# An attention and gated-MLP kernel on one core: block 4's last corner is carried in block 3's empty corner, so that each head makes 12 transposes in place of 13

## The chip, the cores and the metric

The kernel runs on one core of one Trainium2 chip. The metric is the device time of one execution in microseconds (us). The core has five engines that matter here, each with a queue of its own that runs in order: TensorE (PE in the profile; its weight loads are listed apart as PEld), VectorE (DVE), ScalarE (ACT), GpSimd (POOL) and SyncE (SP), which issues all the DMAs.

## What is computed

Attention over 8 batches of 8 heads, each 576 tokens by 64, with a causal mask and a bias that falls with a running sum; then one gated MLP over all tokens of each batch. Cut to what matters:

```python
scores = scale * np.matmul(q, k.transpose(0, 1, 3, 2))
cum = np.cumsum(np.maximum(s, 0.0), axis=-1)
bias = -(cum[:, :, :, None] - cum[:, :, None, :])
scores = np.where(causal, -1000000000.0, scores + np.minimum(bias, 0.0))
attn = np.exp(scores - np.max(scores, axis=-1, keepdims=True))
attn = attn / (np.sum(attn, axis=-1, keepdims=True) + 1e-09)
x = np.matmul(attn, v)                  # heads joined: 8 x 576 x 512
h = gelu(x @ w_in)                      # 8 x 576 x 1024, halves u and v
v_s = w_sg @ (layernorm(v) * g_ln) + b_sg  # over the 576 tokens
return x + (u * v_s) @ w_out
```

## The kernel before

**Blocks of a head.** The 576 query rows of a head are cut into nine groups of 64 and gathered into five blocks, numbered 0 to 4. Block 0 has 64 rows, the others 128. Because of the causal mask, block `it` needs only `ITW[it]` key columns: 64, 192, 320, 448 and 576. Block 4 holds the two last groups of queries: its rows 0 to 63 are the last group and see all 576 keys, its rows 64 to 127 are the group before and see 512. So of the last 64 columns of block 4 only the upper half, 64 x 64, holds anything. This is the corner of which the change speaks. Block 3 is the other way round: its rows 0 to 63 see 384 keys, its rows 64 to 127 see 448. Its buffer is 512 wide (`PW`), with columns 448 to 511 set to zero once at the start. Block 0's 64 x 64 is already put into block 3's rows 0 to 63, columns 384 to 447.

**Steps of a head.** `scores` multiplies queries and keys on PE (lines 295, 297, 298), adds the mask and takes the row minimum on DVE (line 305), takes the exponential with its row sum on ACT (line 315), and calls `norm`. `norm` (lines 318 to 338) adds 1e-9 to the five columns of row sums on ACT (line 320), takes the reciprocal on DVE (line 321) and scales the blocks in the order 3, 0, 2, 1, 4. All of this scaling is on POOL (line 338), but for block 3 of the first 12 heads, which ACT scales (line 336). The scaled blocks stand in `pbuf`, two sets of buffers that heads use in turn.

`transposes` (lines 371 to 430) turns the scaled blocks over, 128 columns at a time, by TensorE transposes against an identity (line 377). It makes four groups for each head, of 4, 4, 2 and 3 transposes. Each group fills one PSUM bank of the tag `pt`, which has two. The last group transposes columns 512 to 575 of block 4 (64 columns, the only narrow transpose), 384 to 511 of block 3 and 384 to 511 of block 4, and then copies the bank out into the tile `pd`. In the first 12 heads (`h < NP`) `pd` is one float32 tile (`pdh`) that two DVE copies fill (lines 420, 421). In the other 52 heads every operand is split into a rounded high part and a low part: ACT casts the high parts (lines 425, 426), and DVE subtracts for the low parts (lines 427, 429).

`pv` (lines 432 to 481) multiplies the transposed blocks with the values: into the bank `xx` (lines 450, 468), and for block 0 into a bank `x0`, which is taken from the two of `pt` (lines 469, 472). The values lie in six tiles of 128 rows. Tile 4 holds the last 64 keys twice, one above the other, and tile 5 the first 64 keys twice.

**The MLP of a batch.** `ffn` splits the attention output and makes units of matmuls of the kinds v, u, s and o (lines 518, 582, 597, 616), whose results are treated by ACT, DVE and POOL. It runs while the next batch's heads run; behind the last batch it runs alone.

**Order.** The steps of heads and MLPs are issued by places in time that are written out by hand (`POS`, `F0`, `F6`, `F7`, `ORDER`). The order of the instructions in each engine's queue is then chosen by the framework, which runs its own model of the timeline over them (`schedule_with_timeline_sim=True`); it also places every wait.

Of the kernel before, what the change touches and what calls it, by code (L numbers as in the profile page):

```python
# [8 lines left out]
F32 = mybir.dt.float32  # L9
# [5 lines left out]
ALU = mybir.AluOpType  # L15

B, H, S, D = 8, 8, 576, 64
# [3 lines left out]
P = 128  # L21
NC = DM // P
NT = 4
REM = S - NT * P
# [35 lines left out]
def tile_attn_gmlp(  # L60
# [12 lines left out]
    nc = tc.nc  # L73
# [9 lines left out]
    def eng(key):  # L83
        return [{"s": nc.scalar, "g": nc.gpsimd, "v": nc.vector}[x] for x in ENG[key]]

    def split(hi, lo, src, eng_hi, eng_lo):
        if eng_hi is nc.scalar:
            nc.scalar.copy(out=hi, in_=src)  # L88
        elif eng_hi is nc.gpsimd:
            nc.gpsimd.tensor_scalar(out=hi, in0=src, scalar1=1.0, scalar2=1.0, op0=ALU.mult, op1=ALU.mult)  # L90
        else:
            nc.vector.tensor_copy(out=hi, in_=src)
        eng_lo.tensor_tensor(out=lo, in0=src, in1=hi.bitcast(F32), op=ALU.subtract)  # L93
# [33 lines left out]
    st = moe.tile([P, 5, BH], F32, name="st", tag="vt", bufs=2)  # L127
# [9 lines left out]
    for c0, n in ((0, 512), (512, REM)):  # L137
        ps = ps_sc.tile([P, 512], F32, name="cps", tag="sc")
        jn = NT if c0 == 0 else 5
        for j in range(jn):  # L140
            k = P if j < NT else REM
            o = max(0, j * P - c0)
# [33 lines left out]
    pbuf = []  # L176
    sums = []
    for i in range(2):
        t = const.tile([66, S], F32R, name=f"q2_{i}")
# [3 lines left out]
        for it in range(5):  # L183
            t = const.tile([P, PW[it]], F32, name=f"p_{i}_{it}")
# [4 lines left out]
        t = const.tile([P, 5], F32, name=f"sum_{i}")  # L189
# [128 lines left out]
    def norm(h, its, rs):  # L318
        c = slice(min(its), max(its) + 1)
        nc.scalar.activation(out=rs[:, c], in_=sums[h % 2][:, c], func=AF.Copy, bias=1e-9)  # L320
        nc.vector.reciprocal(out=rs[:, c], in_=rs[:, c])  # L321
        for it in its:
            r, w = ITR[it], ITW[it]
            p = pbuf[h % 2][it][0:r, 0:w]
            e = eng("n0" if h < NP else "n")[it]


            o = [(p, p, rs[0:r, it:it + 1])]
            if it == 0:
                o = [(pbuf[h % 2][3][0:64, 384:448], p, rs[0:64, 0:1])]  # L330
            elif it == 1:
                o = [(p[:, 0:P], p[:, 0:P], rs[:, 1:2]),
                     (pbuf[h % 2][2][64:P, 256:320], p[64:P, P:192], rs[64:P, 1:2])]
            for po, pi, f in o:
                if e is nc.scalar:
                    nc.scalar.activation(out=po, in_=pi, func=AF.Copy, scale=f)
                else:
                    e.tensor_scalar(out=po, in0=pi, scalar1=f, scalar2=1.0, op0=ALU.mult, op1=ALU.mult)  # L338
# [32 lines left out]
    def transposes(h):  # L371
        d = heads[h]
        pb = pbuf[h % 2]
        pt = {}

        def tr(ps, c, it, jb, n=P):
            nc.tensor.transpose(out=ps[0:n, c:c + P], in_=pb[it][:, jb:jb + n], identity=ident)  # L377

        def new(name, w):
            if h < NP:  # L380
                x = "hl"[h % 2]
                pt[name] = (att.tile([P, w], F32, name=name + x, tag=name + x, bufs=1),)
            else:
                pt[name] = tuple(att.tile([P, w], F32R, name=name + x, tag=name + x, bufs=1) for x in "hl")

        def evac(name, c0, ps, w, e=nc.scalar):
            if h < NP:
                o = pt[name][0][:, c0:c0 + w]
                (e.copy if e is nc.scalar else e.tensor_copy)(out=o, in_=ps[:, 0:w])  # L389
            else:  # L390
                hi, lo = (t[:, c0:c0 + w] for t in pt[name])
                split(hi, lo, ps[:, 0:w], nc.scalar, nc.vector)

        d["pt"] = pt
        t = ps_pt.tile([P, 512], F32, name="pt", tag="pt")
        for c, it in ((128, 3), (384, 2), (0, 1), (256, 4)):
            tr(t, c, it, 0)
        new("pa", 512)
        evac("pa", 0, t, 512)
        yield 0.43  # L400
        t = ps_pt.tile([P, 512], F32, name="pt", tag="pt")
        tr(t, 384, 3, 128)
        tr(t, 0, 3, 256)
        tr(t, 256, 2, 256)
        tr(t, 128, 4, 256)
        new("pb", 768)
        evac("pb", 0, t, 512, nc.vector)
        yield 0.43
        t = ps_pt.tile([P, 512], F32, name="pt", tag="pt")
        tr(t, 128, 2, 128)  # L410
        tr(t, 0, 4, 128)
        evac("pb", 512, t, 256)
        yield 0.43
        t = ps_pt.tile([P, 512], F32, name="pt", tag="pt")
        tr(t, 0, 4, 512, 64)
        tr(t, 64, 3, 384)
        tr(t, 192, 4, 384)
        if h < NP:
            pt["pd"] = (att.tile([P, 320], F32, name="pdh", tag="pdh", bufs=1),)
            nc.vector.tensor_copy(out=pt["pd"][0][0:64, 0:64], in_=t[0:64, 0:64])  # L420
            nc.vector.tensor_copy(out=pt["pd"][0][:, 64:320], in_=t[:, 64:320])
        else:
            hi, lo = pt["pd"] = tuple(att.tile([P, w], F32R, name="pd" + x, tag="pd" + x, bufs=1)
                                      for x, w in (("h", 320), ("l", 192)))
            nc.scalar.copy(out=hi[0:64, 0:128], in_=t[0:64, 0:128])
            nc.scalar.copy(out=hi[:, 128:320], in_=t[:, 128:320])
            nc.vector.tensor_tensor(out=hi[64:128, 0:128], in0=t[0:64, 0:128], in1=hi[0:64, 0:128].bitcast(F32),
                                    op=ALU.subtract)
            nc.vector.tensor_tensor(out=lo, in0=t[:, 128:320], in1=hi[:, 128:320].bitcast(F32), op=ALU.subtract)
        yield 0.35  # L430

    def pv(h):
        d = heads[h]
        pt = d["pt"]
        f32 = h < NP
        c, half = h % H // 2, h % 2
        key = (h // H, c)
        if key not in xr:
            xr[key] = moe.tile([P, S], F32, name="xr", tag="xr", bufs=8)
        xt = xr[key]  # L440
        parts = 1 if f32 else 2
        rows = D if f32 else P

        def st(jt):
            return d["v"][:, jt, :] if f32 else d["vs"][:, jt, :, :].rearrange("p a d -> p (a d)")

        xx = ps_x.tile([P, 512], F32, name="xx", tag="xx")

        def mm(o0, o1, jt, m, **kw):
            nc.tensor.matmul(xx[0:rows, o0:o1], st(jt), m, **{"start": False, "stop": False, **kw})  # L450

        m, pb, pd = pt["pa"], pt["pb"], pt["pd"]
        for k in range(parts):
            mm(0, 512, 0, m[k], start=(k == 0))
        yield 0.2
        for k in range(parts):
            mm(64, 512, 1, pb[k][:, 320:768])
        for k in range(parts):  # L460
            mm(128, 448, 2, pb[k][:, 0:320])
        yield 0.65
        mm(192, 384, 3, pd[0][:, 128:320])
        if not f32:
            mm(192, 384, 3, pd[1])
        x0 = ps_pt.tile([P, 512], F32, name="x0", tag="pt")
        if f32:
            nc.tensor.matmul(xx[0:rows, 256:320], st(4)[0:REM], pd[0][0:REM, 0:64], start=False, stop=True)
            nc.tensor.matmul(x0[0:rows, 0:64], st(0), pd[0][:, 64:128], start=True, stop=True)
        else:  # L470
            mm(256, 320, 4, pd[0][:, 0:64], stop=True)
            nc.tensor.matmul(x0[:, 0:64], st(5), pd[0][:, 64:128], start=True, stop=True)
        hs = slice(64 * half, 64 * half + 64)
        for ps, o, sl in ((x0, slice(0, 64), slice(0, 64)), (xx, slice(0, 512), slice(64, S))):
            if f32:
                nc.scalar.copy(out=xt[hs, sl], in_=ps[0:64, o])
            else:
                nc.scalar.copy(out=xt[hs, sl], in_=ps[64:128, o])
                nc.vector.tensor_tensor(out=xt[hs, sl], in0=ps[0:64, o], in1=xt[hs, sl], op=ALU.add)
        del heads[h]  # L480
        yield 0.5
# [154 lines left out]
    def advance(g, h):  # L636
        if h not in g[1]:
            g[1][h] = g[0](h)
        next(g[1][h], None)

    sc, tr, pp = (scores, {}), (transposes, {}), (pv, {})
    for h in range(BH):
        if h > 0:
# [81 lines left out]
```

## Time and profile before

| | |
|---|---|
| time, median of 3 runs | 828.37 us (827.84 to 835.08) |
| the profiled execution's own time | 830.48 us |
| its span, first to last instruction | 828.8 us |
| mean granted TensorE clock | 0.991 |
| busy, share of the span | PE 96%, PEld 84%, DVE 72%, ACT 70%, POOL 72% |
| instructions | 5161 matmuls, 5161 weight loads, 1806 on DVE, 1620 on ACT, 979 on POOL |

How to read it: the busy shares are of one profiled execution. A matmul's duration is modelled to the end of its pipeline, so that matmuls which follow each other overlap, and what one costs is read from the distance between starts. The chain of waits is followed back from the last instruction, at each step to what released it; its shares say which engine and which line the end of the program hung on.

### The profile page before, as it was taken

What the parts mean: (1) busy time and instruction counts of PE and PEld (TensorE: products, weight loads), DVE (VectorE), ACT (ScalarE), POOL (GpSimd) and SP (SyncE); (2) the same over time, 40 slices, a digit from 0 to 9 for tenths busy, and PEclk for the clock granted to TensorE, in tenths of its full rate; (3) what the DMA queues carried; (4) which work ended last, traced back from release to release, by engine and by line L of the source; (5) the groups of instructions that cost most, each with busy time, mean ns of one, the idle gap of its engine ahead of it and who ended that gap; (6) DMA issues with size and microseconds to landing.
All of it is one profiled execution on the core that took longest, in us unless ns stands there. A gap on an engine that the chain in (4) does not pass through costs nothing.

```text
span 828.8 us, 16733 instructions
## 1 busy us (share of the span) xinstructions
PE 792.6 (96%) x5161; PEld 696.1 (84%) x5161; DVE 597.9 (72%) x1806; ACT 576.5 (70%) x1620; POOL 595.1 (72%) x979
## 2 busy tenths in 40 slices
PE   6899999899999999999989999999999999999878
PEld 3355666889989998999979998899989998899778
DVE  5995468975787578966888577965888678963652
ACT  4787778775686678866878577866787677862430
POOL 4987668878677768796768778785778778872451
PEclk9999999999999999999999999999999999999989
DMA  7656553343442543444434453443444353400101
GB/s 210 215 158 181 148 139 84 86 105 100 116 106 74 128 125 86 108 121 126 112 82 104 115 139 90 113 109 96 119 119 103 100 152 93 98 26 23 35 8 57
DMA packets 69804, 89.29 MB, mean 108 GB/s; under 512 B 25954, under 2 KB 42212, under 8 KB 69716
## 3 DMA queue, kind: packets, MB, share of 16 engines
q1 hardware_dynamic: 69716, 88.23, 40.8%
q8 instruction: 41, 0.67, 0.4%
q14 instruction: 47, 0.39, 0.2%
HBM read 42.27 MB, written 9.73 MB: 63 GB/s over the span
## 4 chain that ended last, share of the span: by engine, by line
PE 73%; DVE 12%; DMA 5%; ACT 3%; issue 3%; POOL 2%; SPq 1%; DVEq 0%; POOLq 0%; ACTq 0%
PE om L616 12%; PE sm L597 11%; PE um L582 10%; PE xx L450 10%; PE vm L518 9%; PE pt L377 8%; PE sc L297 4%; PE sc L298 4%; DVE p L305 2%; DMA xq<-xs 2%; DMA q<-k 2%; PE sm L601 1%; PE sm L600 1%; DVE wbits L220 1%; DVE vm L504 1%
## 5 line engine op out<-in xcount | busy, mean ns | idle before, releaser
L338 POOL TENSOR_SCALAR p<-p,rs 128x448 f32<-128x448 f32 (+4 forms) x372 | 180.5, 499 | 29.1 <-DVE rs L321 9.6
L315 ACT ACTIVATE p<-p,mn 128x448 f32<-128x448 f32 (+4 forms) x320 | 177.9, 557 | 24.5 <-DVE mn L305 22.4
L305 DVE CUSTOM_DVE_ANT_0 p<-sc,mask 64x64 f32<-64x64 f32 (+4 forms) x320 | 126.2, 422 | 56.4 <-PE pt L377 31.0
L377 PE MATMUL pt<-ident,p 128*128 128x128 f32 (+1 forms) x832 | 137.2, 278 | 5.3 <-DVE pbl L389 2.6
L597 PE MATMUL sm<-ws,vn 128*128 128x288 f32 x768 | 130.3, 304 | 0.7 <-POOL vn L567 0.6
L93 POOL TENSOR_TENSOR k<-raw,k 128x576 fp32r<-128x576 f32 x56 | 80.3, 1433 | 66.7 <-ACT k L88 33.3
L582 PE MATMUL um<-xs,wi 128*128 128x288 f32 x768 | 123.4, 300 | 2.5 <-DVE u L504 2.4
L616 PE MATMUL om<-gt,wo 128*128 128x288 f32 x768 | 125.7, 298 | 0.0
L582 PEld LDWEIGHTS um<-xs,wi 128*128 128x128 f32 x768 | 108.9, 188 | 8.9 <-DVE u L504 4.0
L597 PEld LDWEIGHTS sm<-ws,vn 128*128 128x128 f32 x768 | 112.4, 192 | 3.3 <-DVE u L504 1.0
L377 PEld LDWEIGHTS pt<-ident,p 128*128 128x128 f32 (+1 forms) x832 | 96.8, 138 | 21.8 <-DVE pbl L389 5.4
L616 PEld LDWEIGHTS om<-gt,wo 128*128 128x128 f32 x768 | 110.6, 188 | 2.3
L518 PE MATMUL vm<-wi,xs 128*128 128x512 f32 x384 | 103.4, 399 | 0.0
L297 PE MATMUL sc<-k,q 128*128 128x448 f32 x336 | 100.8, 308 | 1.5 <-DVE mn L305 0.8
L298 PE MATMUL sc<-k,q 66*128 66x448 f32 x336 | 89.3, 298 | 0.6 <-DMA k<-cum 0.6
L88 ACT CAST pbh<-pt 128x512 fp32r<-128x512 f32 x104 | 48.9, 479 | 58.8 <-PE pt L377 58.8
L518 PEld LDWEIGHTS vm<-wi,xs 128*128 128x128 f32 x384 | 69.7, 189 | 14.9 <-POOL xs L93 1.6
L93 POOL TENSOR_TENSOR gt<-u,gt 128x288 fp32r<-128x288 f32 x64 | 50.7, 806 | 41.6 <-ACT gt L88 41.1
L297 PEld LDWEIGHTS sc<-k,q 128*128 128x128 f32 x336 | 60.8, 181 | 9.1 <-DVE mn L305 3.9
L93 DVE TENSOR_TENSOR pbl<-pt,pbh 128x512 fp32r<-128x512 f32 x104 | 56.5, 549 | 15.9 <-ACT pbh L88 15.9
L298 PEld LDWEIGHTS sc<-k,q 66*128 66x128 f32 x336 | 60.9, 181 | 5.9 <-issue 0.9
L88 ACT CAST k<-raw 128x576 fp32r<-128x576 f32 x56 | 37.6, 671 | 39.5 <-PE sc L297 33.8
(142 smaller groups left out, 1704.8 us busy)
## 6 DMA issues: line engine op xcount, KB each, us to landing
q<-k SPq DMA_DIRECT2D x168, 144.0 KB
raw<-in_kq SPq DMA_DIRECT2D x56, 288.0 KB
vr<-in_vp SPq DMA_DIRECT2D x52, 192.0 KB
out_t<-ot SPq DMA_DIRECT2D x64, 144.0 KB
k<-k SPq DMA_DIRECT2D x56, 144.0 KB
wraw<-in_w_in SPq DMA_DIRECT2D x16, 256.0 KB
kf<-in_kq SPq DMA_DIRECT2D x8, 288.0 KB
qf<-in_kq SPq DMA_DIRECT2D x8, 288.0 KB
```

The costliest lines, as they stand in the source:

```text
L88: nc.scalar.copy(out=hi, in_=src)
L93: eng_lo.tensor_tensor(out=lo, in0=src, in1=hi.bitcast(F32), op=ALU.subtract)
L297: nc.tensor.matmul(o, d["q1"][:, i0:i0 + r], d["k1"][:, j0:j1], start=True, stop=False)
L298: nc.tensor.matmul(o, q2[h % 2][:, i0:i0 + r], d["k2"][0:66, j0:j1], start=False, stop=True)
L305: nc.vector.tensor_tensor_reduce(out=pbuf[h % 2][it][0:r, j0:j1], in0=pst[0:r, c0:c0 + j1 - j0], in1=(mask2 if it in (2, 4) else mask)[0:r ...
L315: nc.scalar.activation(out=p, in_=p, func=AF.Exp, bias=d["mn"][0:r, it:it + 1], scale=-1.0, accum_out=sums[h % 2][0:r, it:it + 1])
L338: e.tensor_scalar(out=po, in0=pi, scalar1=f, scalar2=1.0, op0=ALU.mult, op1=ALU.mult)
L377: nc.tensor.transpose(out=ps[0:n, c:c + P], in_=pb[it][:, jb:jb + n], identity=ident)
L518: nc.tensor.matmul(ps[0:r], xs[c][:, xi, ts_], wi[:, c, wj, fs], start=(n == 0), stop=(n == 11))
L582: nc.tensor.matmul(ps[:, 0:CH], wi[:, c, wj, dt * P:(dt + 1) * P], xs[c][:, xi, cs], start=(n == 0), stop=(n == 11))
L597: nc.tensor.matmul(ps[:, 0:CH], vn[j][:, vi, ds_], ws[:, j, wj, cs], start=(n == 0), stop=False)
L616: nc.tensor.matmul(ps[:, 0:CH], wo[:, c, wj, ms], gt[ch, c][:, gi, :], start=(n == 0), stop=(n == 11))
```

## The change

In `norm`, block 4 is scaled in two pieces: columns 0 to 511 as before, and the 64 x 64 corner (rows 0 to 63, columns 512 to 575) by an ACT instruction that writes its result into block 3's buffer, rows 0 to 63, columns 448 to 511. In `transposes`, the transpose of block 4's last 64 columns is gone: the transpose of block 3's columns 384 to 511 brings the corner along, and it comes out on partitions 64 to 127 of the PSUM columns 64 to 127, below block 0. The copies out of the bank follow it. In the first 12 heads one DVE copy goes. In the other 52 heads the ACT casts have other shapes (64x64 and 128x256 for 64x128 and 128x192), and the DVE subtraction of 64x128 becomes two of 64x64. In `pv` the first 12 heads multiply the corner from partitions 64 to 127 and block 0 from partitions 0 to 63 alone (values tile 5 for tile 0). Nothing is pinned in the order of the instructions.

```diff
@@ norm
+            elif it == 4:
+                o = [(p[:, 0:512], p[:, 0:512], rs[:, 4:5]),
+                     (pbuf[h % 2][3][0:64, 448:512], p[0:64, 512:S], rs[0:64, 4:5])]
             for po, pi, f in o:
-                if e is nc.scalar:
+                if e is nc.scalar or it == 4 and pi.shape[1] == 64:
                     nc.scalar.activation(out=po, in_=pi, func=AF.Copy, scale=f)
                 else:
                     e.tensor_scalar(out=po, in0=pi, scalar1=f, scalar2=1.0, op0=ALU.mult, op1=ALU.mult)
@@ transposes
-        tr(t, 0, 4, 512, 64)
         tr(t, 64, 3, 384)
         tr(t, 192, 4, 384)
         if h < NP:
             pt["pd"] = (att.tile([P, 320], F32, name="pdh", tag="pdh", bufs=1),)
-            nc.vector.tensor_copy(out=pt["pd"][0][0:64, 0:64], in_=t[0:64, 0:64])
             nc.vector.tensor_copy(out=pt["pd"][0][:, 64:320], in_=t[:, 64:320])
         else:
...
-            nc.scalar.copy(out=hi[0:64, 0:128], in_=t[0:64, 0:128])
-            nc.scalar.copy(out=hi[:, 128:320], in_=t[:, 128:320])
-            nc.vector.tensor_tensor(out=hi[64:128, 0:128], in0=t[0:64, 0:128], in1=hi[0:64, 0:128].bitcast(F32),
+            nc.scalar.copy(out=hi[64:128, 0:64], in_=t[64:128, 64:128])
+            nc.scalar.copy(out=hi[:, 64:320], in_=t[:, 64:320])
+            nc.vector.tensor_tensor(out=hi[0:64, 0:64], in0=t[64:128, 64:128], in1=hi[64:128, 0:64].bitcast(F32),
+                                    op=ALU.subtract)
+            nc.vector.tensor_tensor(out=hi[64:128, 64:128], in0=t[0:64, 64:128], in1=hi[0:64, 64:128].bitcast(F32),
                                     op=ALU.subtract)
             nc.vector.tensor_tensor(out=lo, in0=t[:, 128:320], in1=hi[:, 128:320].bitcast(F32), op=ALU.subtract)
@@ pv
         if f32:
-            nc.tensor.matmul(xx[0:rows, 256:320], st(4)[0:REM], pd[0][0:REM, 0:64], start=False, stop=True)
-            nc.tensor.matmul(x0[0:rows, 0:64], st(0), pd[0][:, 64:128], start=True, stop=True)
+            nc.tensor.matmul(xx[0:rows, 256:320], st(4)[REM:P], pd[0][REM:P, 64:128], start=False, stop=True)
+            nc.tensor.matmul(x0[0:rows, 0:64], st(5)[0:REM], pd[0][0:REM, 64:128], start=True, stop=True)
```

## Prediction

> **What bounds the kernel now.** I read the busy shares first, then the chain of waits by engine, then by line.
>
> ```profile
> span 828.8 us, 16733 instructions
> PE 792.6 (96%) x5161; PEld 696.1 (84%) x5161; DVE 597.9 (72%) x1806; ACT 576.5 (70%) x1620; POOL 595.1 (72%) x979
> ...
> PE 73%; DVE 12%; DMA 5%; ACT 3%; issue 3%; POOL 2%; SPq 1%; DVEq 0%; POOLq 0%; ACTq 0%
> ```
>
> PE is busy nearly throughout and carries 73% of the chain that sets the end. ACT, DVE and POOL are each near 70% busy, so they have room for a little work. But 3% of the chain is ACT and 12% is DVE, so work added there isn't quite free. The chain by line says how much of it is transposes:
>
> ```profile
> by line: PE om L616 12.0%; PE sm L597 10.6%; PE um L582 9.7%; PE xx L450 9.6%; PE vm L518 9.2%; PE pt L377 8.2%; PE sc L297 4.3%; PE sc L298 4.2%; issue 2.7%; DVE p L305 2.0%; DMA xq<-xs 1.9%; DMA q<-k 1.6%; PE sm L601 1.2%; PE sm L600 1.2%
> ...
> L377 PE MATMUL pt<-ident,p 128*128 128x128 f32 x768 | 130.3, 278 | 3.2 <-DVE xr L479 0.9 <-DVE pbl L389 0.8 <-ACT p L336 0.7
> L377 PE MATMUL pt<-ident,p 128*64 128x128 f32 x64 | 17.7, 277 | 2.1 <-DVE pbl L389 1.8 <-DVE pbl L93 0.3
> ```
>
> The second form, 128*64, is the one that goes: 64 of 832. It is as long as the wide form (277 against 278 ns), since both stream 128 columns of the identity. But that is a pipelined duration; the price is the distance to the next start. Three groups of one head, on PE, with what follows each:
>
> ```profile
> 450.64 0.60 PE L377 MATMUL pt<-ident,p 128*128 128x128 f32 x4
> 450.99 0.39 PE L298 MATMUL sc<-k,q 66*128 66x320 f32 x1
> ...
> 452.88 0.38 PE L377 MATMUL pt<-ident,p 128*128 128x128 f32 x2
> 453.02 0.48 PE L450 MATMUL xx<-pal,vs 128*128 128x512 f32 x1
> ...
> 453.86 0.49 PE L377 MATMUL pt<-ident,p 128*64 128x128 f32 x3
> 454.11 1.04 PE L616 MATMUL om<-gt,wo 128*128 128x288 f32 x6
> ```
>
> From the first start to the next matmul: 0.14 us for two, 0.25 for three (the group that loses one), 0.35 for four. So each further transpose costs 0.10 to 0.11 us; I take 0.108. The narrow one fits the same line, so its shape costs nothing beside that.
>
> **What goes.** One transpose for each of 64 heads: 64 x 0.108 = 6.9 us if PE set the pace everywhere. It doesn't: the chain holds 8.2% x 828.8 = 68.0 us of transposes, which is 82 ns for each of the 832. By that, 64 x 0.082 = 5.2 us leave the chain, three quarters of the full price. The other quarter stands where the chain runs over DMA or another engine; there a faster PE only waits longer. I take 5.2, and keep 0 and 6.9 as its ends.
>
> The Trainium skill ("TensorE: Matmul & The Clock Gate", Back-to-back issue gap) gives about 81 ns for one weight load and matmul of 128 columns in a steady stream. By that page the full price would be an estimated 5.2 us, and 3.9 on the chain; the trace has 0.10 to 0.11 us between starts of these float32 transposes, and the measurement decides.
>
> **What is added.** No row shows a 64x64 scaling on ACT. The nearest:
>
> ```profile
> L336 ACT ACTIVATE p<-p,rs 128x448 f32<-128x448 f32 x12 | 8.0, 663 | 1.0 <-DVE rs L321 1.0
> L315 ACT ACTIVATE p<-p,mn 64x64 f32<-64x64 f32 x64 | 21.5, 336 | 0.0
> L478 ACT COPY xr<-xx 64x512 f32<-64x512 f32 x52 | 30.3, 582 | 1.3 <-PE xx L450 0.9
> L478 ACT COPY xr<-x 64x64 f32<-64x64 f32 x52 | 10.8, 208 | 12.0 <-PE x L472 11.1
> L425 ACT CAST pdh<-pt 64x128 fp32r<-64x128 f32 x52 | 13.1, 253 | 9.8 <-PE pt L377 9.1
> L426 ACT CAST pdh<-pt 128x192 fp32r<-128x192 f32 x52 | 16.4, 315 | 0.0
> L427 DVE TENSOR_TENSOR pdh<-pt,pdh 64x128 fp32r<-64x128 f32 x52 | 14.8, 284 | 3.5 <-ACT pdh L426 2.1
> L479 DVE TENSOR_TENSOR xr<-x,xr 64x64 f32<-64x64 f32 x52 | 11.0, 212 | 9.0 <-ACT xr L478 7.9
> L420 DVE COPY pdh<-pt 64x64 f32<-64x64 f32 x12 | 2.5, 208 | 0.0
> L338 POOL TENSOR_SCALAR p<-p,rs 128x576 f32<-128x576 f32 x64 | 49.0, 765 | 0.0
> L566 POOL TENSOR_SCALAR vt<-vt,rt 128x512 f32<-128x512 f32 x32 | 22.3, 695 | 11.0 <-ACT vn L564 11.0
> ```
>
> ACT: the same copy at 512 and at 64 columns takes 582 and 208 ns, 0.835 ns a column. The block scaling of 663 ns, cut by 384 columns, gives 342; the exponential of 64x64, with a per-row operand too, takes 336. I take 340 x 64 = 21.8 us, which brings ACT to 598, 72%. The casts change from 253 + 315 to about 208 (the 64x64 copy) + 368 (315 and 64 columns), some 10 ns more in 52 heads, 0.5 us. Of ACT's 576.5 busy us, 3% of the span, 24.9 us, stands in the chain, so a microsecond of ACT weighs 0.043: (21.8 + 0.5) x 0.043 = 1.0 us. The ends are 0 and all of it, 22.
>
> DVE: two subtractions of 64x64 in place of one of 64x128, by the 64x64 row 2 x 212 - 284 = 140 ns, x 52 = 7.3 us; less the copy, 12 x 208 = 2.5 us. That is 4.8 us more. DVE's weight is 0.12 x 828.8 / 597.9 = 0.166, so 0.8 us; ends 0 and 4.8.
>
> POOL: block 4 at 512 columns in place of 576 saves 70 ns x 64 = 4.5 us; its weight is 0.02 x 828.8 / 595.1 = 0.028, so -0.1 us. The narrower float32 multiplications of `pv` I put at 0, since these rows of 64 and 128 operand rows differ by 4 ns:
>
> ```profile
> L469 PE MATMUL x<-pdh,vf 128*64 128x64 f32 x24 | 3.9, 246 | 0.0
> L468 PE MATMUL xx<-pdh,vf 64*64 64x64 f32 x24 | 3.9, 242 | 0.0
> ```
>
> No DMA is issued more, less or later in its queue.
>
> **The waits that are added.** The transpose of block 3's last columns now waits for ACT's corner, and all of PE's queue behind it with it. One head shows the cover:
>
> ```profile
> 439.58 0.19 DVE L321 RECIPROCAL rs<-rs 128x5 f32<-128x5 f32 x1
> 440.59 3.46 POOL L338 TENSOR_SCALAR p<-p,rs 128x448 f32<-128x448 f32 x6
> ...
> 446.90 0.66 PE L377 MATMUL pt<-ident,p 128*128 128x128 f32 x4
> ```
>
> The reciprocal is there at 439.77, POOL scales until 444.05, and this head's first group starts at 446.90; the group that needs the corner is the one at 453.86. ACT has 14 us for 0.34 us of work, so PE's new wait costs nothing. Were that cover gone, PE would wait up to the 0.34 us in each head. The later subtraction in front of `pv` has a cover too:
>
> ```profile
> L427 DVE TENSOR_TENSOR pdh<-pt,pdh x52: 283/284/285, 148.6 to 760.1; 64x128 fp32r<-64x128 f32 x52
> ...
> who waited for it (us, times):
>   PEld x L472: 0.5, 1
>   PE x L472: 0.3, 1
> ```
>
> PE waited once in 52 heads for it, 0.3 us. With 0.14 us more it stays nearly always early. The bank is held 0.14 us longer as well, but all 832 transposes together had only 3.2 + 2.1 us of idle PE ahead of them.
>
> **The sum.** -5.2 + 1.0 + 0.8 - 0.1 = -3.5 us. Against the profiled execution's 830.48 us (span 828.8, with 1.7 around it) that is 827.0. This execution lay 0.25% above the median of 828.37, so against the median I say **824.9 us**, -0.4%. About 1% is what a measurement of this kernel can tell from no change.
>
> **The order is chosen anew.** The framework plans by its own model, and an instruction more on ACT and one less on PE can change its choices anywhere in the program. How much an order can be worth is seen inside this run. The same group of twelve matmuls opens each batch's stretch in the chain:
>
> ```profile
> 337.58 1.84 PE um L582 x12
> ...
> 433.48 1.85 PE um L582 x12
> ...
> 526.99 1.85 PE um L582 x12
> ...
> 620.63 1.85 PE um L582 x12
> ...
> 713.93 1.85 PE um L582 x12
> ```
>
> The stretches are 95.9, 93.5, 93.6 and 93.3 us, with eight heads and one MLP in each. So one order can cost 2.4 us a batch more than another; over the five batches from 246 to 714 us that is 12 us either lost, or, for the one slow stretch here, 2.4 us won.
>
> **The rivals.** *Nothing arrives* (0.2): the freed PE time turns into longer waits for DMAs and DVE, and the added 1.8 us of ACT and DVE stay: 830 us. For it speaks the 17% of the chain that DMA and DVE hold; against it, PE's 73%. The change not doing what it says is this case too: if the planner keeps a hole where the transpose stood, the time is the same.
>
> *All of it and more* (0.2): PE is the pace everywhere, the additions are covered: 828.4 - 6.9 = 821.5. With the slow stretch mended too it is 819.1, 1.1% faster. For it speaks PE's 96%, and that PE idled only 3.2 + 2.1 us ahead of all transposes. Against it, the chain holds 82 ns of each transpose and not 108, and each order that mends one stretch can spoil another.
>
> *ACT's queue is blocked* (0.15), on the other side. The corner needs the reciprocal, which is DVE's, and which itself needs ACT's sums. If the planner puts the corner right behind those sums, ACT stands until DVE comes to the reciprocal, and behind it stand the exponentials and the evacuations of PSUM that PE needs. The existing scaling does this:
>
> ```profile
> 65.83 0.20 ACT L320 ACTIVATE rs<-sum 128x5 f32<-128x5 f32 x1
> 66.06 0.19 DVE L321 RECIPROCAL rs<-rs 128x5 f32<-128x5 f32 x1 [2.51 <-ACT rs L320]
> 66.29 0.68 ACT L336 ACTIVATE p<-p,rs 128x448 f32<-128x448 f32 x1 [0.26 <-DVE rs L321]
> ```
>
> ACT idled 0.26 us for it here, with a DVE that was free at once. The Trainium skill (the same page, on engine queue depths) says that ACT and DVE are strictly first in, first out, and that only PE's weight loads pass ahead; the wait in this row agrees. A corner would block ACT for 0.26 + 0.34 = 0.60 us a head. It turns the sum at 5.2 / 64 = 0.08 us of that on the chain, and makes the kernel 1% slower at 0.21 us (13.5 us in all, of which 8.3 remain): 837 us. With all 0.60 it would be 38 - 5.2 = 33 us slower, 861. The same sign and size comes from the slow order in all batches (12 - 3.5 = 8.5 us), which is why I let 0.15 stand for both. Against it: the 14 us of room let the planner place the corner after the reciprocal.
>
> **How the numbers follow.** Forecast 0.45, nothing arrives 0.2, all and more 0.2, blocked 0.15. The forecast's own range is 822 to 829. For 8 in 10 I go from 818.5, below the second rival, to 836, leaving out most of the third. Faster by over 1% (under 820.1) needs all of the gain and a better order: 0.15 of the second rival's 0.2. Slower by over 1% (over 836.7) is the blocked ACT or the slow order in most batches: 0.13. Within 1%: 0.72.
>
> **What the profile after should show.** PE's transposes x768 and no 128*64 form; ACT with 64 new scalings of 64x64 at about 340 ns and little idle time ahead of them; POOL's block 4 at about 695 ns; DVE's 64x64 subtractions at about 212; the two-transpose group 0.14 us to the next start; steady stretches 8 x 0.108 = 0.9 us shorter, less 8 x 1.7 / 64 = 0.2 for what is added: about 92.8. PE idle ahead of the last group <-ACT would show the new wait, and stretches of 95 or 96 us a worse order. The prediction is wrong if order moves more than the 3.5 us of the sum.

## The result: 0.9% slower, and the profile after

The changed kernel takes 836.02 us (median of 20 runs, 831.37 to 840.84) against 827.88 for before (20 runs): 1.0091 times as long, 95% interval 1.0076 to 1.0106 (the two medians alone give 1.0098). The forecast was 0.4% faster. The page of the changed kernel has the span, the busy shares and the chain of waits by engine:

```profile
span 834.6 us, 16753 instructions
PE 791.4 (95%) x5097; PEld 693.6 (83%) x5097; DVE 604.4 (72%) x1846; ACT 599.6 (72%) x1684; POOL 590.9 (71%) x979
...
PE 71%; DVE 10%; DMA 8%; ACT 5%; issue 3%; POOL 2%; SPq 1%; POOLq 0%; DVEq 0%
```

64 matmuls are gone and PE's busy time fell by only 1.2 us, not by the 6 or 7 that 64 transposes are worth. So its other matmuls kept it busy longer. DMA and ACT gained in the chain (5 to 8%, 3 to 5%). The instructions themselves, in the groups by line and form, are what the prediction priced:

```profile
L339 ACT ACTIVATE p<-p,rs 64x64 f32<-64x64 f32 x64 | 21.9, 342 | 6.7 <-DVE rs L321 6.6
...
L426 ACT CAST pdh<-pt 64x64 fp32r<-64x64 f32 x52 | 10.8, 208 | 14.7 <-PE pt L380 13.5
L427 ACT CAST pdh<-pt 128x256 fp32r<-128x256 f32 x52 | 19.4, 374 | 0.6
...
L428 DVE TENSOR_TENSOR pdh<-pt,pdh 64x64 fp32r<-64x64 f32 x52 | 11.8, 226 | 6.0 <-ACT pdh L427 4.6
L430 DVE TENSOR_TENSOR pdh<-pt,pdh 64x64 fp32r<-64x64 f32 x52 | 11.3, 218 | 0.7
...
L341 POOL TENSOR_SCALAR p<-p,rs 128x512 f32<-128x512 f32 x64 | 44.7, 698 | 0.0
...
L380 PE MATMUL pt<-ident,p 128*128 128x128 f32 x768 | 132.6, 280 | 6.3 <-DVE pbl L392 1.5
```

The corner takes 342 ns where 340 was said, POOL's block 698 where 695 was said, and the subtractions 226 and 218 where 212 was said. The narrow transposes are gone and 768 are left. ACT idled 6.7 us in all ahead of the corner, a tenth of a microsecond a head and not the 0.26 of the rival. PE waited for the corner once, 0.7 us. The loss is in none of these rows.

**Where it is.** The view by cores gives the granted clock of each span, before first:

```profile
core 0: 828.8 us, clock 0.991
```

```profile
core 0: 834.6 us, clock 0.985
```

0.006 of 830 us is 5.0 us, most of the 5.8 by which the spans differ (an estimate, as if PE set the pace wherever the clock was low). The view by windows (stretch, its length, each engine's busy time and count, then PEclk, DMA share and GB/s) shows where the clock goes. First before, then after:

```profile
418.20:421.60 3.40, 1.58 (x10) 1.29 (x10) 0.75 (x2) 1.90 (x7) 2.31 (x4) 1.00 0.14 29
421.60:425.00 3.40, 3.40 (x13) 2.75 (x12) 2.63 (x10) 1.86 (x7) 0.05 (x1) 0.50 0.00 0
```

```profile
247.10:250.50 3.40, 2.46 (x10) 1.27 (x11) 3.40 (x11) 3.40 (x12) 2.40 (x5) 1.00 0.34 96
250.50:253.90 3.40, 3.40 (x14) 3.07 (x14) 3.25 (x13) 1.76 (x7) 0.64 (x3) 0.51 0.00 0
260.80:264.20 3.40, 2.06 (x11) 1.27 (x9) 3.26 (x12) 2.17 (x9) 1.01 (x3) 1.00 0.41 104
264.20:271.00 6.80, 6.23 (x27) 6.04 (x28) 3.11 (x9) 3.41 (x9) 2.83 (x3) 0.50 0.33 75
```

Behind a stretch of 3.4 us in which PE stands for a good part, the next 3.4 us can run at half clock, and matmuls in them take longer. Before has 13.7 us at half clock (one stretch in the steady part, at 421.6, the others at 155 and 800). After has 23.9 us, three of its stretches between 250 and 350 us. Counted by matmuls done (transposes left out), the changed kernel is 1.1 us ahead of before at 220 us, 6.3 behind at 265, 8.9 behind at 354 and 5.9 at the end. So in these two executions the loss is made where those three stretches lie. The Trainium skill ("TensorE: Matmul & The Clock Gate", Part 1) tells of a free-running window of 3413 ns and half rate after one idle window; the lengths agree (3.4 and 6.8 us), but here a window with 1.58 or 2.46 us of work in it was enough.

What made PE stand at 262 us is in the chain and in PE's timeline of after:

```profile
257.44 4.74 DMA q<-k
262.18 0.02 issue
262.19 0.26 SPq L285
...
262.51 2.22 DMA vnr<-vnr
```

```profile
264.77 0.61 PE L604 MATMUL sm<-wr,vnr 66*128 66x288 f32 x1 [1.88 <-DMA vnr<-vnr]
```

SP's queue is in order: k<-cum (line 285) waits for the transfers of the head, the transfer of vnr (line 569 before, 572 after) stands behind it, and PE waits 1.88 us for that. No instruction of the change is in these rows. What the change did there is that it gave the framework's planner, the model that chooses the order, other instructions to place: the order of the matmuls differs from before's in hundreds of places, from the first heads on.

### The profile page after: what moved, and what is told of

The parts are those of the page before. It is cut to its first block, busy times and chain, and to the rows that moved or that the text cites. A ratio compares the mean times of both kernels' runs of the same rounds, so it can differ in the third digit from the quotient of the medians.

```text
span 834.6 us, 16753 instructions
## 1 busy us (share of the span) xinstructions
PE 791.4 (95%) x5097; PEld 693.6 (83%) x5097; DVE 604.4 (72%) x1846; ACT 599.6 (72%) x1684; POOL 590.9 (71%) x979
## 4 chain that ended last, share of the span: by engine, by line
PE 71%; DVE 10%; DMA 8%; ACT 5%; issue 3%; POOL 2%; SPq 1%; POOLq 0%; DVEq 0%
PE om L619 11%; PE sm L600 10%; PE um L585 10%; PE vm L521 9%; PE xx L453 9%; PE pt L380 7%; PE sc L297 4%; PE sc L298 4%; DMA q<-k 3%; DVE p L305 2%; DMA xq<-xs 2%; PE sm L604 1%; PE sm L603 1%; ACT p L315 1%; DVE wbits L220 1%
## 5 line engine op out<-in xcount | busy, mean ns | idle before, releaser
L341 POOL TENSOR_SCALAR p<-p,rs 128x448 f32<-128x448 f32 (+4 forms) x372 | 174.6, 483 | 29.6 <-DVE rs L321 11.9
L380 PE MATMUL pt<-ident,p 128*128 128x128 f32 x768 | 132.6, 280 | 6.3 <-DVE pbl L392 1.5
L585 PE MATMUL um<-xs,wi 128*128 128x288 f32 x768 | 125.3, 304 | 1.5 <-DVE u L507 0.7
L600 PE MATMUL sm<-ws,vn 128*128 128x288 f32 x768 | 124.9, 302 | 1.2 <-POOL vn L570 0.7
L585 PEld LDWEIGHTS um<-xs,wi 128*128 128x128 f32 x768 | 112.1, 193 | 5.4 <-DVE u L507 1.8
L380 PEld LDWEIGHTS pt<-ident,p 128*128 128x128 f32 x768 | 91.3, 141 | 23.8 <-DVE pbl L392 4.5
L93 POOL TENSOR_TENSOR vs<-vr,vs 128x384 fp32r<-128x384 f32 x52 | 53.3, 1024 | 16.4 <-ACT vs L88 11.2
L93 DVE TENSOR_TENSOR pbl<-pt,pbh 128x512 fp32r<-128x512 f32 x104 | 56.0, 548 | 10.9 <-ACT pbh L88 10.6
```

The costliest lines, as they stand in the source:

```text
L585: nc.tensor.matmul(ps[:, 0:CH], wi[:, c, wj, dt * P:(dt + 1) * P], xs[c][:, xi, cs], start=(n == 0), stop=(n == 11))
L600: nc.tensor.matmul(ps[:, 0:CH], vn[j][:, vi, ds_], ws[:, j, wj, cs], start=(n == 0), stop=False)
```

## The experiments

Each ratio is against before on the same chip, with its 95% interval; 0.1% is 0.83 us. Clocks averaged over a kernel's runs are from the list of its runs.

**Theory A: a new order. Theory B: the corner in ACT's queue.** To part the instructions from their order, some kernels have every engine's queue order held: instructions that follow each other in the wanted order get an edge that only orders their issue. On one in-order queue that should add no wait; no run holds before in its own order and does nothing else, so what the holding costs is not measured by itself.

```python
seq = ...   # one engine's instructions in the order of the other kernel
for a, b in zip(seq, seq[1:]):
    tc.add_manual_dep(b, a.name, info)   # NoSync: order of issue only
```

*The whole change in before's order:*

> All of the change, but every engine's queue is held in the order that the kernel before has (the two subtractions stand where the one stood, ACT's corner stands right ahead of the head's first evacuation, the fourth transposes are simply missing). Theory A, the new order: what the change itself does is worth about the sum of the prediction, and the loss comes from the order that the planner chose anew. Then 821 to 825 us, 3 to 7 faster than before, at a granted clock of about 0.991 as before. Theory B, ACT's queue: the corner blocks ACT in whatever order. Then 832 to 838 us.

*Before's instructions in the changed kernel's order:*

> None of the change: the kernel before, instruction for instruction, but with every engine's queue in the order that the changed kernel has (the transpose and the copy that the changed kernel lacks stand right ahead of their neighbours). Theory A, the new order: as slow as the changed kernel and 64 transposes more, 836 + 5 = 838 to 843 us, with a granted clock below 0.990. Theory B, ACT's queue: the cause is gone, 826 to 830 us.

*The planner left free, and one part of the change alone:* the transposes without the corner (`elif it == 4` taken out of `norm`), which leaves the last 64 keys of block 4 out of the result, and the corner alone, scaled on ACT in its place with 13 transposes (`p[0:64, 512:S]` as the output).

> Of the change the transposes and the copies alone, order left to the planner: POOL scales all 576 columns of block 4 and no ACT corner is issued; the last 64 keys of block 4 are left out of the result. Theory A, the new order: again a new order, so the time can lie anywhere from 822 to 838, and does not tell what a transpose costs. Theory B, ACT's queue: the price of the transposes without ACT, 822 to 825 us.

> Of the change ACT's corner alone, order left to the planner: block 4's corner is scaled by ACT in its place, POOL scales 512 columns, and all 13 transposes stay. Theory A, the new order: anywhere from 826 to 840 us. Theory B, ACT's queue: 836 to 843 us, with the same idle time of ACT ahead of the corner as in the changed kernel (6.7 us).

| kernel | us | ratio |
|---|---|---|
| change, before's order | 826.89 | 1.0006 (0.9987 to 1.0026) |
| before, change's order | 836.31 | 1.0128 (1.0101 to 1.0155) |
| transposes alone, free | 848.28 | 1.0275 (1.0239 to 1.0310) |
| corner alone, free | 831.91 | 1.0077 (1.0049 to 1.0105) |

Before slows to the changed kernel's time when it is only put in its order, with not one instruction of the change. Its profile shows the low clock too:

```profile
core 0: 834.6 us, clock 0.988
```

The change in before's order costs nothing. Theory B falls, and of A the main point holds: the loss comes with the order. The transposes alone, the part that takes work off PE, gave the slowest kernel of all when the planner was free. But three of A's numbers were missed. The held order brought no gain (821 to 825 us expected). Before in the changed kernel's order took 836.31 us and not 838 to 843. The transposes alone took 848.28, over the 838 at which A had ended.

The clock is a part of what an order costs, not all of it. The corner alone ran at a mean clock of 0.993, as before did beside it, and was still 0.8% slower. Before in the changed kernel's order ran at 0.989 against 0.993: an estimated 3.7 of its 10.6 us.

**Is it the change, or any new order?** Two kernels with before's instructions. In each, one of the hand-written numbers is altered by which the MLP's steps are placed in time ahead of the planner:

```diff
-CV = 1.4
+CV = 1.3
```

```diff
-MT = 52.0
+MT = 51.0
```

> Before's instructions, not one changed; one number that the planner is given for a v unit's first half (CV) is 1.3 instead of 1.4, so that the order comes out another way. Theory A (a new order by itself moves the time by more than the 3.5 us of the predicted sum): over 3.5 us away from before's 827, more likely slower, 831 to 845. Rival (orders of the planner lie within 2.4 us of each other, as the prediction had it from the batches): 825 to 830.

> Before's instructions, not one changed; another number of the planner (MT, 51.0 instead of 52.0). Theory A: over 3.5 us away from before's 827, more likely slower, 831 to 845. Rival: 825 to 830.

They took 840.07 us (1.0161, 1.0133 to 1.0189) and 833.40 us (1.0068, 1.0043 to 1.0092), at clocks of 0.988 and 0.985 in the profiled runs. Each of the five orders that were drawn anew is slower than before's, by 0.7 to 2.8%; in these two, not one instruction differs. So the change's 0.9% lies within what a redrawn order costs by itself.

**Theory C: ACT's corner eats the gain in the held order. Theory D: PE's gain turns into waiting.** All in before's order: the transposes without the corner; the corner with 13 transposes; the corner later in ACT's queue; the corner on POOL.

> In the order of the kernel before, the change without ACT's corner (POOL scales all 576 columns of block 4; the last 64 keys of block 4 are left out of the result). With the order held the whole change came out at 826.9 us against 826.4, so 64 x 0.109 = 7.0 us of PE went somewhere. Theory C, ACT's corner ate it: without the corner the gain is there, 820 to 822 us. Theory D, PE's gain turns into waiting for DVE, ACT and DMA whatever ACT does: 825 to 827 us.

> In the order of the kernel before, ACT's corner alone: scaled in its place right ahead of the head's first evacuation, POOL scales 512 columns, all 13 transposes stay. Theory C, ACT's corner costs what the transposes bring: 831 to 833 us. Theory D, the corner lies in ACT's idle time: 826 to 828 us.

> All of the change in the order of the kernel before, but in the last 52 heads ACT's corner stands right ahead of the second evacuation (the 512 columns of pbh), where ACT idles 22.4 us in the kernel before, and not of the first. Theory C, the corner's place in ACT's queue decides: 821 to 824 us. Theory D: 826 to 828 us, no difference to the other place.

> All of the change in the order of the kernel before, but the corner is scaled by POOL right behind the rest of block 4, as an instruction of its own of some 0.33 us, and ACT has none. Theory C, ACT's time was the price: 820 to 823 us, if POOL's additional 64 x (0.33 - 0.07) = 17 us stay beside the path. Theory D: 825 to 828 us.

| held order | us | ratio |
|---|---|---|
| 12 transposes, no corner | 826.89 | 1.0008 (0.9988 to 1.0027) |
| 13 transposes, corner on ACT | 829.17 | 1.0027 (1.0011 to 1.0043) |
| whole, corner ahead of the second evacuation | 829.44 | 1.0029 (1.0006 to 1.0052) |
| whole, corner on POOL | 831.39 | 1.0061 (1.0040 to 1.0083) |

Beside 13 transposes the corner costs 2.2 us (0.9 to 3.6), whatever the holding costs included. Beside 12 it costs nothing that can be measured (1.0006 whole, 1.0008 without the corner). On POOL it costs more. Three of the four times (829.17, 829.44 and 831.39 us) lie in the range of neither theory. But the transposes alone bring nothing, which is D. With the order held, the traces of before and of the kernel with 12 transposes and no corner can be laid beside each other matmul by matmul. Each missing transpose does bring the following starts forward by 0.10 to 0.11 us; with small losses between, they stand at -1.01 us at 174 us and at -1.81 at 320, eleven transposes later. Then, once or twice a batch, it is given back at one place: by 0.8 us at 324, 0.8 at 445, 0.5 at 517 and 1.3 at 700. At 445 and 517 PE waits there for one of two transfers (vnr 0.55 us, xq 0.44). At 324 and 700 it stands ahead of a matmul that reads xq too, but the profile puts these waits down to DVE (0.52 and 1.22 us). Both transfers stand in the chain of this kernel:

```profile
503.43 3.63 DMA q<-k
...
508.11 3.63 DMA xq<-xs
...
531.85 2.20 DMA vnr<-vnr
```

xq (line 528) is the input of the v unit for a batch's last 64 tokens, and vnr that unit's result. On SP's queue both stand behind the transfers of a head, whose own waits come from ACT and POOL. So a PE that is early at xq would only wait longer.

**Take the wait away.** The four xq transfers are put ahead of the head's q<-k on SP's queue, with and without the change:

```python
to = max(j for j in range(at) if names[j] in MARK["qk"])   # the head's first q<-k
names[to:at + 8] = four + rest                             # xq ahead of it
```

> Before in its own order, held, with the same move of the four transfers xq<-xs on SP's queue and nothing else. PE's idle time ahead of the L532 matmuls that was put down to xq<-xs is 6.7 us in five places. Theory D: that time comes back in part, 822 to 825 us (before 827). Rival E: 826 to 830.

> The whole change in before's held order, and on SP's queue the four transfers xq<-xs of a batch's last 64 tokens now stand ahead of the q<-k transfers of the same head instead of between and behind them (six batches). Theory D (in the held order the transposes' gain ends at PE's wait for these transfers, +0.7 to +1.3 us each time): the waits go, 820 to 824 us, 3 to 6 us under the same kernel without the move (826.89) and under before. Rival E (the four transfers now hold up the q<-k transfers behind them by 2.5 us, and PE waits for those in their place): 826 to 830, no gain over 826.89.

Before with the move took 824.59 us (0.9967, 0.9952 to 0.9982), in D's range. The change with it took 827.50 (1.0009, 0.9988 to 1.0030), in the rival's. In PE's timeline, before and then before with the move:

```profile
417.17 1.08 PE L582 MATMUL um<-xs,wi 128*128 128x288 f32 x7
420.07 0.50 PE L532 MATMUL vm<-wi,xq 128*128 128x512 f32 x1 [1.82 <-DMA xq<-xs]
...
423.57 0.44 PE L298 MATMUL sc<-k,q 66*128 66x288 f32 x1
```

```profile
416.23 1.08 PE L659 MATMUL um<-xs,wi 128*128 128x288 f32 x7
417.15 0.39 PE L609 MATMUL vm<-wi,xq 128*128 128x512 f32 x1
...
419.62 0.29 PE L374 MATMUL sc<-k,q 66*128 66x288 f32 x1
```

In the second trace the wait of 1.82 us is gone, and so is the half clock behind it: the same matmul of scores takes 0.29 us and not 0.44, and between 410 and 429 us the trace gains 3.0 us. But the move is not the reason. The kernel with 13 transposes and the corner on ACT has the same order with xq not moved, and it gains 2.95 us in the same stretch. What differs is on SP's queue, in before and then in that kernel, and last PE's wait in the latter:

```profile
416.02 3.27 SPq L528 DMA_DIRECT2D xq<-xs  x3
```

```profile
415.34 1.97 SPq L598 DMA_DIRECT2D xq<-xs  x3
...
419.66 0.49 PE L602 MATMUL vm<-wi,xq 128*128 128x512 f32 x1 [0.29 <-DMA xq<-xs]
```

One of the three issues took 1.92 us in before's profiled execution, where the median of its 32 is 0.63. In the five kernels that have this order and xq in its place, none of the 32 takes over 0.70, and PE waits at most 0.3 us at this place. So this slow stretch of before, on which the prediction had built, belongs to that one execution as far as the record shows. From one batch's first o matmul to the next's it has 95.8 us in before, 93.7 with the corner and no move, and 92.5 with the move.

What the move does is seen between the two kernels without the corner, with xq in its old place and moved: 826.89 and 824.07 us (1.0008 and 0.9960). The second trace gains 0.8 us at 322 and 1.5 at 695, two of the places where the transposes' gain had been given back. The clock has no part in the move's gain: over 12 runs, before with the move has a mean clock of 0.993, as before has beside it.

For the changed kernel the move did not help, though not by the wait for q<-k that E named. Beside its control it loses 1.0 us at one sm<-ws,vn in each of five batches. ACT, DVE and PE there, first the control and then the change:

```profile
342.71 0.59 ACT L163 CAST pah<-pt 128x512 fp32r<-128x512 f32 x1
...
343.33 0.69 DVE L168 TENSOR_TENSOR pal<-pt,pah 128x512 fp32r<-128x512 f32 x1 [0.35 <-ACT pah L163]
...
344.90 0.68 DVE L643 TENSOR_SCALAR vt<-vt,rt 64x512 f32<-64x512 f32 x1
345.50 0.44 DVE L580 SCALAR_TENSOR_TENSOR u<-u,um 128x288 f32<-128x288 f32 x1
...
346.00 1.87 PE L674 MATMUL sm<-ws,vn 128*128 128x288 f32 x12
```

```profile
342.85 0.33 ACT L415 ACTIVATE p<-p,rs 64x64 f32<-64x64 f32 x1
343.21 0.59 ACT L163 CAST pah<-pt 128x512 fp32r<-128x512 f32 x1
...
343.82 0.69 DVE L168 TENSOR_TENSOR pal<-pt,pah 128x512 fp32r<-128x512 f32 x1 [0.59 <-ACT pah L163]
...
345.39 1.10 DVE L655 TENSOR_SCALAR vt<-vt,rt 64x512 f32<-64x512 f32 x1
346.43 0.43 DVE L592 SCALAR_TENSOR_TENSOR u<-u,um 128x288 f32<-128x288 f32 x1
...
346.91 1.86 PE L686 MATMUL sm<-ws,vn 128*128 128x288 f32 x12 [0.92 <-DVE u L592]
```

The corner makes pah 0.50 us late, pah makes DVE's subtraction 0.49 late, one DVE instruction takes 1.10 us at its later place and not 0.68, and the last product of the gelu, whose PSUM bank sm needs, is 0.93 late. PE waits 0.92. In the groups by line, this wait of sm<-ws,vn for u grew from 0.4 to 4.9 us. What made the one DVE instruction longer is not known.

**Theory F: the corner is what gives the gain back. Rival G: any wait takes it.** Three more in the held order with xq moved: no corner; the corner in those five heads ahead of the third evacuation; and this, with vnr's transfer put ahead of the k<-cum in front of it.

> Before's held order with the four transfers xq<-xs moved ahead, 12 transposes and the changed copies, but the corner on ScalarE left out (the last 64 keys of block 4 do not reach the output). Against the same order and move with 13 transposes (824.59): Theory F (the transposes' price is 0.1 us each, and in this order it is ScalarE's corner that gives it back, through pah, the pal subtraction and the gelu's last product to the bank that sm<-ws,vn waits for): 818 to 821. Rival G (the missing transposes only bring PE sooner to waits that stand anyway): 823.5 to 826.

> The whole change with the same move of xq<-xs; in five of the 64 heads (28, 36, 44, 52, 60: the one head in each of five batches ahead of whose sm<-ws,vn PE loses about 1.0 us) ScalarE's corner stands ahead of the third evacuation (pbh, 256 columns) instead of ahead of the first (pah). Theory F: 5 x 0.9 = 4.6 us of the 827.5 come back: 821 to 824.5, under before and under before with the move alone (824.59). Rival G: another wait takes the place, 826 to 829.

> The same as the run with five corners moved, and on SP's queue the transfer of vnr stands ahead of the k<-cum in front of it (it is issued up to 1.0 us sooner, once a batch). PE's idle time put down to vnr<-vnr is 0.7 us in two places of the profile with the corners at their first place, and more once those waits are gone. Theory F: 0 to 2 us under the run without this move. Rival: k<-cum comes later and PE waits for it in its place, same or 1 us more.

And the controls for the last one, without the change and without the corner:

> Before in its own held order with both moves on SP's queue (xq<-xs ahead of the head's q<-k, vnr ahead of the k<-cum in front of it), 13 transposes. It is the control of the changed kernel with the same two moves and five corners moved (823.09). Theory F (with these waits gone the transposes' 0.1 us each arrive): 826 to 828, 3 us or more over 823.09. Rival G (the next wait takes them): 822 to 825, within 2 us of it.

> The same order and moves with 12 transposes and without ScalarE's corner (the last 64 keys of block 4 do not reach the output). Theory F: 819 to 821. Rival G: 822 to 825, within 1.5 us of its control with 13 transposes.

| held order | xq moved | xq and vnr moved |
|---|---|---|
| 13 transposes (before) | 824.59, 0.9967 (0.9952 to 0.9982) | 823.61, 0.9962 (0.9947 to 0.9977) |
| 12, no corner | 824.07, 0.9960 (0.9939 to 0.9981) | 820.92, 0.9933 (0.9918 to 0.9949) |
| whole, five corners later | 826.54, 0.9985 (0.9961 to 1.0010) | 823.09, 0.9947 (0.9925 to 0.9968) |

F missed: without the corner, the transposes brought 0.5 us against their control. G had it. The groups by line of the control and of the kernel without the corner show who took it:

```profile
L674 PE MATMUL sm<-ws,vn 128*128 128x288 f32 x768 | 129.3, 302 | 1.0 <-POOL vn L644 0.7 <-DVE u L580 0.4
...
L678 PE MATMUL sm<-wr,vnr 66*128 66x288 f32 x64 | 19.1, 314 | 0.6 <-DMA vnr<-vnr 0.5
```

```profile
L683 PE MATMUL sm<-ws,vn 128*128 128x288 f32 x768 | 129.0, 302 | 2.1 <-DVE u L589 1.4
...
L687 PE MATMUL sm<-wr,vnr 66*128 66x288 f32 x64 | 19.1, 313 | 2.1 <-DMA vnr<-vnr 2.1
```

The wait for vnr went from 0.5 to 2.1 us and that for u from 0.4 to 1.4. With five corners later the first rose to 3.5; that profiled run was the slowest of its 12 (831.78 us, median 826.54), at a clock of 0.987:

```profile
L692 PE MATMUL sm<-wr,vnr 66*128 66x288 f32 x64 | 19.4, 318 | 3.5 <-DMA vnr<-vnr 3.5
```

```profile
core 0: 830.0 us, clock 0.987
```

With vnr moved too, that wait is 0.0, and the time 3.5 us lower, where 0 to 2 were expected:

```profile
L698 PE MATMUL sm<-wr,vnr 66*128 66x288 f32 x64 | 18.9, 311 | 0.0
```

Now something arrives: without the corner 0.9933 against 0.9962 for its control, about 2.4 us, though the intervals of these ratios still overlap. Run against run on their chip it is 2.6 us, with a 95% interval of 1.3 to 3.9. The control fell in G's range (822 to 825 us), the kernel without the corner in F's (819 to 821). The whole change (0.9947) is not parted from its control (0.9962). Both, at 823.1 and 823.6 us, lie under before and under the changed kernel. This gain comes from the two moves on SP's queue; that the change adds to it is not shown.

## Why the prediction was wrong

- **The step that failed is the one on the order.** The text said that the prediction is wrong if order moves more than the 3.5 us of the sum, and it did: before's own instructions in the changed kernel's order took 1.28% longer, 10.6 us. I had put the forecast at no effect of the order, with the stretches of before's batches as a measure of how far orders differ. But those stretches are batches of one plan, and their spread says nothing of another plan. The one slow stretch of them, 95.9 us, was no order at all: it was one late xq, with the half clock behind it, in one execution. The slow order in all batches had a share in a chance of 0.15. Five of five redrawn orders were slower. The other way round, in the new order, the change lies 0.4% under before's instructions (1.0091 against 1.0128), but the intervals overlap.
- **I did not read the clock.** It stood in the table at 0.991, and nothing in the sum could change it. About 5 of the 8 us lost are clock, by the estimate above. In after's 20 runs time and clock go together (correlation -0.85; 831.37 us at 0.994, 840.84 at 0.979).
- **The transposes, -5.2: mis-sized.** The price of 0.10 to 0.11 us a piece is right, and each one came. But its share of the chain was taken for the part that stays. In the held order nothing stayed (+0.08%, -0.12 to +0.27), and some 2.4 us did once two late transfers were moved. The rival *nothing arrives* had this mechanism and its price.
- **The corner, +1.0: it has no one price.** It measured +2.2 us (0.9 to 3.6) beside 13 transposes, nothing beside 12, and about 4 us beside 12 with xq moved (1.0009 against 0.9960). ACT's weight of 0.043 was a mean; the corner stands at the head of pah, pal and gelu, where in five heads each tenth counts. The cover of the new wait of the transposes held, as said, but for 0.7 us in one head.
- **The blocked ACT** (837 us) gave nearly the right time for the wrong reason: the corner idled ACT 0.1 us a head.
- DVE's +0.8 and POOL's -0.1 were not tried alone.
- That a measurement tells about 1% from no change was too modest: with 20 runs the interval is 0.15% to either side.

Left open: why a redrawn order tends to be slower than before's. An obvious candidate is that before's hand-written numbers were chosen because their order was a fast one; no run here tests that. Open too is what part of PE's standing within a 3.4 us window decides on the half clock. In before's trace the window from 780.0 has 1.70 us of PE work and none follows it, while in after's one with 2.57 us, from 342.7, has.

## What to carry to other kernels

Where a planner draws the order, a change of one instruction has two effects, its own and that of the redraw; hold the order to see the first, and redraw it without the change to see the size of the second. A share of the chain says where time is spent now, not what is saved by spending less: ask where the faster engine stops next, which here was above all one of two transfers in an in-order queue, once a batch. Read the granted clock by windows before stretches are compared, and look for a stretch in a second trace before a forecast is built on it.

## What was not expected of the hardware

A wait of PE far shorter than 3.4 us can have a half-clock stretch of 3.4 us behind it: in before's trace, 1.82 us at xq. The trace without both was 3.0 us ahead in that stretch. The starts of the half-clock stretches of one run lie whole multiples of 3.413 us apart (4.0 and 28.0 of them in after, from 250.5 to 264.2 and 346.1). It may therefore matter where a wait falls on that grid; no run here tests it. And one execution can have a slow DMA issue of its own: 1.92 us for one xq, where the median was 0.63. Five of the other traces, all of them in another order on SP's queue, have one xq issue of 1.27 to 1.75 us. The cause is unknown.
